# First batch's DFT stage on 64x64 tiles of TensorE, with its loads put in another order (spectral mixing followed by a tanh-shrink MLP)

## The chip, the cores and the metric

One Trainium2 chip, one core. The metric is the device time of one launch in microseconds, the median of several runs. Before the change it is 2542.09 us (three runs, 2541.68 to 2546.36).

## The reference

The input x has 8 batches of 3008 positions and 256 channels. Each batch is filtered along the positions in the frequency domain, and every resulting row then goes through an MLP whose nonlinearity is h - tanh(h):

```python
X = np.fft.rfft(x, axis=1)
Y = X * (filt_r + 1j * filt_i)[None, :, :]
y = np.fft.irfft(Y, n=3008, axis=1).reshape(8 * 3008, 256)
h = y @ w_in                      # 256 -> 2048
out = (h - np.tanh(h)) @ w_out    # 2048 -> 256
```

## The kernel before, in words

The DFT of length 3008 = 64 x 47 is done by matrix products. A position is 47 q + r, with q from 0 to 63. Stage one takes, for a residue r from 0 to 23, the 64 rows of x at r (lower partitions 0 to 63) and the 64 rows at 47 - r (upper partitions 64 to 127), and multiplies them by a table of cosines and sines. Stage two mixes the residues ("there", tiles `pq`, `pa`, `pb`), the filter is multiplied in (tiles `nn`, `xy`), and the way back (`pe`, `pu`) gives the rows that the MLP reads. Batch 0 does all of this in a prologue of some 76 us. The batches after it are prepared in steps that are put between the MLP's matmuls of the batch ahead of them, so that from there to the end TensorE has MLP work in a fixed order written out by the program.

The prologue's start is what the change touches:

- **Loads** (L1172 to L1187). For each of three chunks `c` of 8 residues there is a tile `xs[c]` of 128 partitions x 8 slots x 256 channels. SyncE's queue loads the table piece `fh` of chunk 0 and all lower halves; GpSimd's queue loads all upper halves but the first, which with the other two table pieces is on ScalarE's queue. Slot i of the upper half holds residue 47 - r, so it is read backwards from memory, one row of 1 KB at a time.
- **Table** (L1188, L1189). VectorE builds `f0`, 128 columns for each residue: the 64 columns of `fh`, and beside them the same columns with the sign of the upper rows turned.
- **Warmers** (L1200). 15 matmuls of 128x256 on a tile of ones, without use for the result.
- **Stage one** (`first0`, L1064 to L1074). For each residue and each half of the channels one full matmul: 128 rows (lower and upper at once), 128 channels as weights, 128 columns of `f0` moving. So the sum over lower and upper rows is made in the array, and the difference, which the sign in `f0` gives, too. Each PSUM bank of two residues is copied to the tile `turnt` (which is laid in the memory of `wd`), by ScalarE for ten of the twelve.
- **What follows.** `across(0)` (L1083 to L1100) transposes slices of `turnt`, over all residues, into `pq`; its first slice lies in the columns 64 to 127. ScalarE and VectorE then copy `pq`, and a row of VectorE work follows almost without a pause: conversion of the MLP's weights (L183 to L201, from a tile `raw`), the sums of stage two (L435, L436) and the filter (L447 to L456).
- **Filters.** GpSimd copies one element of `xs[2]` (`gate`, L1197), which waits for a piece of the last chunk, and only then issues the loads of the first filter tiles.

The loads of SyncE's and ScalarE's queues share eight completion counters in turn, so a later load of these queues is issued only when the load that had its counter before it has landed.

## Time and profile before

| what | time |
|---|---|
| median of three runs | 2542.09 us |
| the profiled execution's own time | 2542.18 us |
| its span, first to last instruction | 2540.3 us |
| TensorE busy in the span | 2522.6 us (99%) |
| granted TensorE clock, mean | 0.999 |
| first matmul of stage one | 10.72 us |
| first transpose behind stage one (`pq`) | 22.54 us |
| first matmul of the way back's last step (`pu`) | 76.05 us |

The span is 1.9 us less than the time of that execution. Times in rows of the trace are microseconds from the start of the span. An f32 matmul stands in the trace as two records on PE (and two on PEld, its weight loads), so 15 matmuls are 30 records.

### The profile page before, as it was taken

Reading aid. Unit: us, or ns where it says so; the run is one execution under the profiler, and the core shown is the slowest. Engines: PE = TensorE matmul, PEld = TensorE weight load, DVE = VectorE, ACT = ScalarE, POOL = GpSimd, SP = SyncE. Lnnn points to the kernel's source line nnn. Section 1 sums busy time; section 2 is a strip of 40 time slices with the busy share of each in tenths; the row PEclk is TensorE's granted clock in tenths of the full one; section 3 lists DMA queues with packets and bytes.
Section 4 is the critical chain, followed back from the end, with each engine's and each line's share of the span. In section 5 each row is a group of like instructions: output and inputs, shape, how many; then the busy total and the mean of one; then the engine's idle time right before and its main releaser. Section 6 shows DMA issues by size and latency. Waiting matters only on the chain.

```text
span 2540.3 us, 44575 instructions
## 1 busy us (share of the span) xinstructions
PE 2522.6 (99%) x17072; PEld 2173.1 (86%) x17072; DVE 1935.6 (76%) x2270; ACT 1694.2 (67%) x2551; POOL 1532.0 (60%) x1112
## 2 busy tenths in 40 slices
PE   9999999999999999999999999999999999999998
PEld 8678889888898888988888888898889888898887
DVE  6888877988678876888669886698866888555555
ACT  4666666667666766676667666666666666666665
POOL 5255665667556765676656665666655666455552
PEclk9999999999999999999999999999999999999999
DMA  9854224422343323342334322343123322110110
GB/s 245 261 150 117 65 54 100 112 65 53 86 108 91 82 69 89 80 112 59 80 87 105 87 56 72 96 111 89 36 72 84 92 66 53 26 31 19 25 22 19
DMA packets 333664, 211.37 MB, mean 83 GB/s; under 512 B 231645, under 2 KB 305531, under 8 KB 329793
## 3 DMA queue, kind: packets, MB, share of 16 engines
q1 hardware_dynamic: 319091, 184.93, 29.8%
q0 software_dynamic: 11120, 16.16, 2.3%
q10 hardware_dynamic: 3230, 7.34, 0.9%
q8 instruction: 136, 2.23, 0.4%
q14 instruction: 87, 0.71, 0.1%
HBM read 127.81 MB, written 83.39 MB: 83 GB/s over the span
## 4 chain that ended last, share of the span: by engine, by line
PE 96%; DVE 2%; DMA 1%; issue 0%; POOL 0%; ACT 0%; ACTq 0%; SPq 0%; POOLq 0%; DVEq 0%
PE o L821 44%; PE x L648 25%; PE z L648 12%; PE y L648 6%; PE pm L415 2%; PE pu L595 2%; PE pm L351 1%; PE o L883 1%; PE pf L308 1%; DMA filt<-in_filt_r_dram 1%; DMA x<-in_x_dram 0%; DMA ct<-e 0%; PE o L719 0%; PE x L719 0%; PE z L719 0%
## 5 line engine op out<-in xcount | busy, mean ns | idle before, releaser
L821 PE MATMUL o<-t,wd 128*128 128x256 f32 (+1 forms) x3008 | 762.7, 376 | 0.0
L619 POOL TENSOR_TENSOR t<-h 128x512 f32<-128x512 f32 (+1 forms) x184 | 303.6, 1650 | 707.3 <-DVE h L771 642.2
L771 DVE TENSOR_TENSOR h<-h,y 128x1024 f32<-128x1024 f32 (+1 forms) x384 | 571.0, 1487 | 156.4 <-ACT y L767 156.4
L821 PEld LDWEIGHTS o<-t,wd 128*128 128x128 f32 x3008 | 568.8, 190 | 84.5 <-POOL o L853 15.1
L648 PE MATMUL x<-tu,wu 128*128 128x256 f32 (+1 forms) x2256 | 571.4, 376 | 0.0
L821 PE MATMUL o<-h,wd 128*128 128x256 f32 (+1 forms) x2256 | 569.9, 375 | 0.2 <-DVE h L771 0.2
L648 PEld LDWEIGHTS x<-tu,wu 128*128 128x128 f32 x2256 | 427.4, 190 | 53.8 <-issue 3.9
L821 PEld LDWEIGHTS o<-h,wd 128*128 128x128 f32 x2256 | 428.3, 190 | 50.9 <-issue 0.8
L654 ACT COPY s<-x 128x512 f32<-128x512 f32 (+1 forms) x188 | 109.3, 581 | 517.4 <-PE x L648 517.3
L764 ACT ACTIVATE y<-y 128x1024 f32<-128x1024 f32 (+1 forms) x384 | 399.5, 1040 | 12.1
L767 ACT ACTIVATE y<-y 128x1024 f32<-128x1024 f32 (+1 forms) x384 | 399.8, 1041 | 4.6
L761 ACT ACTIVATE y<-h 128x1024 f32<-128x1024 f32 (+1 forms) x384 | 400.6, 1043 | 2.5 <-DVE h L697 1.7
L622 POOL TENSOR_TENSOR t<-h,t 128x512 f32<-128x512 f32 (+1 forms) x184 | 338.3, 1838 | 0.0
L620 POOL TENSOR_TENSOR t<-h,t 128x512 f32<-128x512 f32 (+1 forms) x184 | 310.5, 1688 | 14.4
L621 POOL TENSOR_TENSOR t<-h 128x512 f32<-128x512 f32 (+1 forms) x184 | 276.9, 1505 | 0.0
L654 ACT COPY u<-x 128x512 f32<-128x512 f32 (+1 forms) x376 | 214.1, 569 | 72.9 <-PE x L648 69.6
L697 DVE COPY h<-x 128x512 f32<-128x512 f32 (+1 forms) x188 | 127.6, 679 | 129.1 <-PE x L648 128.9
L689 DVE TENSOR_TENSOR h<-z,u 128x512 f32<-128x512 f32 (+1 forms) x188 | 127.2, 677 | 88.9 <-ACT u L654 88.5
L648 PE MATMUL x<-ut,wu 128*128 128x256 f32 (+1 forms) x752 | 194.0, 380 | 0.2 <-DVE h L697 0.2
L648 PE MATMUL z<-tu,wu 128*128 128x256 f32 (+1 forms) x752 | 190.2, 375 | 1.4 <-DVE h L705 1.4
L648 PE MATMUL y<-ut,wu 128*128 128x256 f32 (+1 forms) x752 | 190.1, 375 | 0.0
L648 PE MATMUL z<-ut,wu 128*128 128x256 f32 (+1 forms) x752 | 190.0, 375 | 0.0
(215 smaller groups left out, 2933.5 us busy)
## 6 DMA issues: line engine op xcount, KB each, us to landing
ft<-filt SPq DMA_DIRECT2D x28, 1024.0 KB
ct<-nn SPq DMA_DIRECT2D x56, 512.0 KB
e<-ct SPq DMA_DIRECT2D x47, 512.0 KB
a<-ct SPq DMA_DIRECT2D x112, 192.0 KB
out_dram<-ot SPq DMA_DIRECT2D x1248, 16.0 KB
x_sb<-in_x_dram SPq DMA_DIRECT2D x110, 128.0 KB
ct<-a SPq DMA_DIRECT2D x60, 128.0 KB
ct<-x_sb SPq DMA_DIRECT2D x60, 128.0 KB
```

The source lines that it names most:

```text
L619: by.tensor_sub(t[0], b[0][1], b[0][0])
L620: by.tensor_sub(t[1], b[1][1], t[0])
L621: by.tensor_sub(t[2], b[1][1], b[0][1])
L622: by.tensor_sub(t[3], b[1][0], t[1])
L648: nc.tensor.matmul(bank[:, k], wu[:, q - 1, (2 * u + k) * 128:(2 * u + k + 1) * 128], rhs[q - 1], start=(first and k == 0), stop=True, ski ...
L654: ACT.copy(t, X)
L697: V.tensor_copy(h[:, 2, :, 0:w], X)
L761: ACT.activation(y[k], ht[k], AF.Arctan, scale=TURN)
L764: ACT.activation(y[k], y[k], AF.Tanh, scale=BEND)
L767: ACT.activation(y[k], y[k], AF.Square, scale=SCALE, accum_out=y_sums[:, 2 * U + k // 2:2 * U + k // 2 + 1])
L771: V.tensor_mul(ht[k], ht[k], y[k])
L821: nc.tensor.matmul(product(q), wd[:, q - 1, (2 * u + k) * 128: (2 * u + k + 1) * 128], rhs[q - 1][:, k], start=(u == 0 and k == 0 and q == ...
```

## The change

Stage one of batch 0 works on quarters of the array. A matmul now has 64 rows, 64 channels as weights and 64 moving columns of `fh`; four of them, one in each quarter, take the place of one. The products of lower rows go to one PSUM bank and those of upper rows to another. ScalarE copies the upper bank to a tile `upper`, and VectorE writes sum and difference of the two to `turnt`. Since the upper rows are apart, slot 3 - k of an upper half can be paired with slot k of the lower half, so the upper halves are read forwards (3 or 4 KB at a time). The table is loaded as `fh`, 64 columns for each of the 24 residues; `f0` is left for the 8 residues that a later step of batch 1 needs, and built by ScalarE. The loads stand in the order of their use on SyncE's and ScalarE's queues, GpSimd loads no part of x any more, and `gate` looks at a piece that SyncE's queue loads. Six warmers stand ahead in place of 15, on ones in the memory of `wu`, and two more behind each half chunk but the last.

```diff
-                for i in range(0, 8, 2):
-                    r = 8 * c + i
-                    pf = z0("pf", [128, 2, 2, 128])
+                for at in (0, 4):
+                    r = 8 * c + at
+                    banks = [z0("pf", [128, 2, 4, 64]) for _ in range(2)]
                     for h in range(2):
-                        for k in range(2):
-                            nc.tensor.matmul(pf[:, h, k], xs[c][:, i + k, h * 128:h * 128 + 128],
-                                             f0[:, r + k], start=True, stop=True)
-                    copy = V.tensor_copy if c == 2 and i % 4 else ACT.copy
-                    copy(turnt[:, :, :, r:r + 2], pf.rearrange("p h k n -> p h n k"))
+                        for k in range(4):
+                            for bank, half, slot in zip(banks, rows, (at + k, at + 3 - k)):
+                                for m, part in enumerate(rows):
+                                    col = h * 128 + 64 * m
+                                    nc.tensor.matmul(bank[part, h, k],
+                                                     xs[c][half, slot, col:col + 64],
+                                                     fh[half, r + k], start=True, stop=True)
+                    if r < NH - 4:
+                        warmer(2, ones_t)
+                    t = tr.tile([128, 2, 4, 64], F32, tag="e1", bufs=2, name="upper")
+                    ACT.copy(t, banks[1])
+                    low, high = (v.rearrange("p h k n -> p h n k") for v in (banks[0], t))
+                    V.tensor_add(turnt[:, :, 0:64, r:r + 4], low, high)
+                    V.tensor_sub(turnt[:, :, 64:128, r:r + 4], low, high)
...
-                V.tensor_copy(f0[:, r:r + 8, 0:64], fh)
-                V.tensor_scalar(out=f0[:, r:r + 8, 64:128], in0=fh,
-                                scalar1=sgn, scalar2=None, op0=ALU.mult)
...
+            load_f(0, 8, nc.sync)
+            load_high(0, 0, ACT)
+            load_low(0, 0, nc.sync)
+            load_high(0, 4, ACT)
+            load_low(0, 4, nc.sync)
+            load_f(8, NH, ACT)
+            for k in (0, 4):
+                load_high(1, k, ACT)
+            for k in (0, 4):
+                load_low(1, k, nc.sync)
+            for k in (0, 4):
+                load_low(2, k, nc.sync)
+                load_high(2, k, nc.sync)
...
-            warmer(15, filt[2][:, 0])
+            warmer(6, ones_t)
             first0(0)
+            ACT.copy(f0[:, :, 0:64], fh[:, 0:8])
+            ACT.copy(f0[0:64, :, 64:128], fh[0:64, 0:8])
+            ACT.mul(f0[64:128, :, 64:128], fh[64:128, 0:8], -1.0)
             first0(1)
```

On TensorE, the program's start before the change reads as follows (`pf` is stage one's bank, `x_87`, `x_97`, `x_106` are the three chunks, `f_80` is `f0`; xN counts matmuls in a row):

```order
L1081 MATMUL warm<-filt_79 128x256 x15
L1071 MATMUL pf<-f_80,x_87 128x128 x16
L1071 MATMUL pf<-f_80,x_97 128x128 x16
L1071 MATMUL pf<-f_80,x_106 128x128 x16
L1094 MATMUL pq<-one_sb,wd 120x128 x8
```

And with the change, up to the second chunk (`x_85`, `x_86`, `x_87` are the chunks now):

```order
L1090 MATMUL warm<-wu 128x256 x6
L1074 MATMUL pf<-fh,x_85 64x64 x32
L1090 MATMUL warm<-wu 128x256 x2
L1074 MATMUL pf<-fh,x_85 64x64 x32
L1090 MATMUL warm<-wu 128x256 x2
L1074 MATMUL pf<-fh,x_86 64x64 x32
```

Nine warmers have gone from the front, ten stand between the half chunks, and each half chunk has 32 quarter matmuls where it had 8 full ones.

On VectorE, ahead of the first copy of `pq`, this stood last before the change:

```order
L1188 COPY f_80<-fh 128x8x64
L1189 TENSOR_SCALAR f_80<-fh,sgn 128x8x64
L1188 COPY f_80<-fh 128x8x64
L1189 TENSOR_SCALAR f_80<-fh,sgn 128x8x64
L1074 COPY wd<-pf 128x256x2 x2
L1099 COPY a_68<-pq 120x512
```

With the change the end of the same stretch is:

```order
L1082 TENSOR_TENSOR wd<-pf,upper 128x2x64x4
L1083 TENSOR_TENSOR wd<-pf,upper 128x2x64x4
L1082 TENSOR_TENSOR wd<-pf,upper 128x2x64x4
L1083 TENSOR_TENSOR wd<-pf,upper 128x2x64x4
L1108 COPY a_68<-pq 120x512
```

The building of the table has left VectorE, and for each half chunk a sum and a difference have come, twelve instructions in all (`wd` is the memory of `turnt`).

On SyncE's queue the loads of x and of the table now begin like this, where GpSimd had the upper halves before:

```order
L1183 DMA fh_81<-f 128x512
L1186 DMA x_85<-in_x_dram 64x1024 x2
L1186 DMA x_86<-in_x_dram 64x1024 x2
L1186 DMA x_87<-in_x_dram 64x1024
L1191 DMA x_87<-in_x_dram 64x1024
L1186 DMA x_87<-in_x_dram 64x1024
L1191 DMA x_87<-in_x_dram 64x1024
L1208 DMA one_sb<-one 128x128
L1209 DMA mats_sb<-mats 120x360
```

Two upper halves have come ahead of the identity `one_sb`, the matrices `mats_sb` and all that follows on this queue; the other upper halves stand on ScalarE's queue.

More of the change, by code (lines that the diff above doesn't have):

```diff
@@ L1162 @@
             filt = [pro.tile([KM, 4, DM], F32, name=f"filt{k}") for k in range(3)]
-            f0 = pro.tile([128, NH, 128], F32, name="f0")
+            f0 = pro.tile([128, 8, 128], F32, name="f0")
+            fh = pro.tile([128, NH, 64], F32, name="fh")
             warm_b = cst.tile([128, 1], F32, name="warm_b")
@@ L1166 @@
             jobs = parts_of((0, 1, 2, 4, 3, 5, 6, 7))
-            sgn = cst.tile([128, 1], F32, name="sgn")
-            for half in range(2):
-                V.memset(sgn[64 * half:64 * half + 64], 1.0 - 2 * half)
-            V.memset(filt[2][:, 0], 1.0)
-            xs, began = [], []
-            for c in range(3):
-                lo = int(c == 0)
-                xt = big([128, 8, DM], F32, "x0")
-                xs.append(xt)
-                fh = pro.tile([128, 8, 64], F32, tag="e1", bufs=4, name="fh")
-                (ACT if c else nc.sync).dma_start(fh, f_d[:, 512 * c:512 * c + 512])
-                if lo:
-                    V.memset(xt[64:128, 0], 0.0)
-                for k in (0, 4):
-                    nc.sync.dma_start(xt[0:64, k:k + 4], dram(x.tensor, (8 * c + k) * DM,
-                                                              [[NR * DM, 64], [1, 4 * DM]]))
-                    at = max(k, lo)
-                    (ACT if c + k == 0 else G).dma_start(
-                        xt[64:128, at:k + 4], dram(x.tensor, (NR - 8 * c - at) * DM,
-                                                   [[NR * DM, 64], [-DM, k + 4 - at], [1, DM]]))
-                r = 8 * c
-                V.tensor_copy(f0[:, r:r + 8, 0:64], fh)
-                V.tensor_scalar(out=f0[:, r:r + 8, 64:128], in0=fh,
-                                scalar1=sgn, scalar2=None, op0=ALU.mult)
@@ new lines, with load_f, load_low @@
+            ones_t = wu[:, 6, 0:256]
+            V.memset(ones_t, 1.0)
+            xs, began = [big([128, 8, DM], F32, "x0") for _ in range(3)], []
+            V.memset(xs[0][64:128, 3], 0.0)
+            def load_f(a, b, queue):
+                queue.dma_start(fh[:, a:b], f_d[:, 64 * a:64 * b])
+            def load_low(c, k, queue):
+                queue.dma_start(xs[c][0:64, k:k + 4], dram(x.tensor, (8 * c + k) * DM,
+                                                           [[NR * DM, 64], [1, 4 * DM]]))
@@ new lines, in load_high @@
+            def load_high(c, k, queue):
+                n = 4 - (c + k == 0)
+                queue.dma_start(xs[c][64:128, k:k + n],
+                                dram(x.tensor, (NR - 8 * c - k - 3) * DM,
+                                     [[NR * DM, 64], [1, n * DM]]))
+            load_f(0, 8, nc.sync)
[6 more added lines that the diff above has]
+                load_high(1, k, ACT)
```

## Prediction

> **What bounds the kernel now.** I read the page first (its head, the busy shares and the chain that ended last), then a table of four stretches.

> ```profile
> span 2540.3 us, 44575 instructions
> PE 2522.6 (99%) x17072; PEld 2173.1 (86%) x17072; DVE 1935.6 (76%) x2270; ACT 1694.2 (67%) x2551; POOL 1532.0 (60%) x1112
> PE 96%; DVE 2%; DMA 1%; issue 0%; POOL 0%; ACT 0%; ACTq 0%; SPq 0%; POOLq 0%; DVEq 0%
> ```

> The chain is TensorE nearly all the way. The table says where it isn't (columns: PE, PEld, DVE, ACT, POOL busy, clock, DMA share, GB/s):

> ```profile
> 24.00:40.00 16.00, 14.93 (x82) 12.37 (x82) 15.45 (x25) 8.90 (x16) 6.87 (x11) 1.00 0.84 222
> 40.00:56.00 16.00, 15.33 (x78) 12.86 (x79) 15.19 (x21) 6.87 (x13) 12.32 (x15) 1.00 0.84 233
> 56.00:76.00 20.00, 17.62 (x90) 15.08 (x88) 17.65 (x32) 7.74 (x15) 1.67 (x3) 1.00 0.69 227
> 76.00:2440.00 2364.00, 2362.08 (x16208) 2034.59 (x16209) 1826.42 (x2108) 1603.35 (x2413) 1461.54 (x1029) 1.00 0.33 81
> ```

> From 76 to 2440 us TensorE is busy for 2362.08 of 2364 us, on work whose order is fixed. So whatever the prologue wins or loses by 76 us moves the end by as much. From 24 to 56 us VectorE is busy for 30.6 of 32 us: an earlier first copy of `pq` pulls that whole row of work forward, if its data are there. The question is then when `pq` begins, and whether that lead lives to 76 us. The timeline of the start (start, us, engine, line):

> ```profile
> 1.45 9.44 PE L1081 MATMUL warm<-filt 120*128 120x256 f32 x30 [1.45 <-DVE filt L1170]
> 10.72 10.88 PE L1071 MATMUL pf<-f,x 128*128 128x128 f32 x96
> 19.96 1.58 ACT L1074 COPY wd<-pf 128x512 f32<-128x512 f32 x2 [1.10 <-PE pf L1071]
> 21.64 0.80 DVE L1074 COPY wd<-pf 128x512 f32<-128x512 f32 x1 [0.99 <-PE pf L1071]
> 22.54 1.06 PE L1094 MATMUL pq<-one_sb,wd 128*120 128x128 f32 x8 [0.94 <-ACT wd L1074]
> ```

> Warmers until 10.7 us, stage one's 96 records without a gap until 21.6, one last copy of 0.80 us, then `pq` at 22.54. In that stretch TensorE sets the pace, not the loads:

> ```profile
> 2.00:4.00 2.00, 2.00 (x6) 1.58 (x5) 0.00 (x0) 1.35 (x2) 2.00 (x5) 1.00 0.97 258
> 4.00:6.00 2.00, 2.00 (x6) 1.53 (x6) 1.36 (x2) 0.13 (x1) 2.00 (x4) 1.00 0.95 206
> 6.00:8.00 2.00, 2.00 (x9) 1.68 (x8) 0.00 (x0) 0.00 (x0) 0.48 (x2) 1.00 1.03 294
> 8.00:10.00 2.00, 2.00 (x11) 1.77 (x10) 0.00 (x0) 0.00 (x0) 0.00 (x0) 1.00 1.01 291
> 10.00:12.00 2.00, 2.00 (x17) 1.90 (x16) 0.82 (x2) 0.18 (x1) 0.00 (x0) 1.00 1.05 304
> 12.00:14.00 2.00, 2.00 (x21) 2.00 (x20) 0.00 (x0) 1.81 (x3) 0.00 (x0) 1.00 1.04 291
> 14.00:16.00 2.00, 2.00 (x21) 2.00 (x20) 0.82 (x2) 1.80 (x3) 0.60 (x2) 1.00 1.06 264
> ```

> Two things are to be seen. The same warmer goes at 6 records in 2 us at first and at 11 later, though the clock column shows 1.00: TensorE starts at half pace. The chain has the later pace of matmuls with 256 columns:

> ```profile
> 41.33 0.43 PE pe L1139 x2
> ```

> That is 0.215 us a record, and 0.43 at half of it. 12 cold and 18 warm records make 5.2 + 3.9 = 9.1 us, and 0.2 for the first one the 9.27 us from 1.45 to 10.72: the pace turns near 6.7 us. And the DMA engines are full (share near 1); two microseconds times each GB/s give 0.52, 0.93, 1.52, 2.10, 2.71, 3.29, 3.82 MB moved by 4, 6, 8, 10, 12, 14 and 16 us.

> **The change, part by part.**

> *Start.* The warmers wait for a memset of VectorE as before, a little earlier; six are 12 records at the cold pace, 12 x 0.43 = 5.2 us with 0.1 to 0.2 for the first, from 1.2 to 6.5 us. The first half chunk needs the table piece and the first two x pieces:

> ```profile
> 4.20 0.62 DVE L1188 COPY f<-fh 128x512 f32<-128x512 f32 x1 [2.42 <-DMA fh<-f]
> 6.82 0.33 SPq L1191 DMA_DIRECT2D one_sb<-one  x1
> 15.40 0.19 POOL L1197 COPY gate<-x 1x1 f32<-1x1 f32 x1 [8.91 <-DMA x<-in_x_dram]
> ```

> The table piece had landed by 4.20. The load of `one_sb` had to wait for the counter of the first lower half, so that one landed by 6.8. In the new order it has the same place behind the same piece, so I take 6.8 us for stage one's start, where it was 10.72.

> *Matmuls.* Quarters of the same shape run later in this kernel:

> ```profile
> 110.83 1.67 PE L719 MATMUL x<-ut,wu 128*128 128x448 f32 x4
> 112.33 1.67 PE L883 MATMUL o<-h,wd 128*128 128x448 f32 x4
> ...
> 118.57 1.67 PE L719 MATMUL o<-ut,wu 128*128 128x448 f32 x4
> 120.17 1.16 PE L595 MATMUL pu<-gt,e 64*64 64x64 f32 x64
> 121.26 1.77 PE L883 MATMUL o<-h,wd 128*128 128x448 f32 x4
> ```

> 64 records, 32 quarter matmuls, from 120.17 to the next group at 121.26 are 1.09 us, and 0.1 at the way in (1.60 from the start of the group before it, where its like at 110.83 has 1.50): 1.18 us, which is one half chunk. It had 8 full matmuls, 16 of the 96 records in 10.88 us, 1.81 us. Two warmers are 4 x 0.215 = 0.86 us. So a half chunk with its warmers is 2.04 us, and six of them less the last warmers are 11.4 us, where the 96 records took 10.9: the quarters save 3.8 us and the ten warmers give 4.3 back. The lead is that of the start.

> *Loads.* x and the table are 3.87 MB, and nothing else is on the queues before the last of them but what I name below. If SyncE's and ScalarE's queues share evenly, the second chunk's first half needs the fourth load of ScalarE's queue, 1.25 MB on that queue and 2.49 MB in all: 11.3 us on the table above, where TensorE would be there at 6.8 + 2 x 2.04 = 10.9. It waits 0.4 us. The next halves need all 1.51 MB of ScalarE's queue and as much of SyncE's (3.0), then SyncE's seventh load (3.3) and all 3.87 MB: 13.0, 14.2 and 16.2 us, where TensorE comes at 13.3, 15.4 and 17.4. So they don't wait, and stage one ends at 17.4 + 1.2 = 18.6 us (before: 21.6). Reading forwards makes larger packets; in the rows, the GB/s don't show me a gain beyond that from 258 to 304, worth some 0.3 us on the half megabyte that had 1 KB packets on ScalarE's queue, and I count nothing.

> *Evacuation.* The tail behind the last matmul grows: a copy by ScalarE, then a sum and a difference by VectorE, where it was one copy. The rows of the like steps (min/median/max ns):

> ```profile
> L601 ACT COPY odd<-pu x48: 577/586/588, 77.9 to 2463.8; 128x512 f32<-128x512 f32 x48
> L605 DVE TENSOR_TENSOR ut<-pu,odd x11: 690/692/693, 78.6 to 2464.4; 128x512 f32<-128x512 f32 x11
> L605 DVE TENSOR_TENSOR ut<-even,odd x37: 864/1506/1751, 215.7 to 2101.8; 128x512 f32<-128x512 f32 x37
> L606 DVE TENSOR_TENSOR ut<-even,odd x37: 1214/1756/1764, 217.0 to 2103.3; 128x512 f32<-128x512 f32 x32, 128x384 f32<-128x384 f32 x5
> ```

> With one operand in PSUM, as here, 0.69 us. The writes to `turnt` go in short runs, and the copy that wrote there so took 0.80 (the timeline above), so I take 0.75, with 0.69 and 1.76 (both operands in SBUF) as the ends. Tail: 0.59 + 0.05 + 2 x 0.75 = 2.1 us, against 0.80. Ahead of the last half, VectorE's 1.5 us fits under the 2.04 us that TensorE takes, and so do ScalarE's 0.59 us and its three builds of `f0` (some 1.8 us between the second and the third copy, which has 2.5 us of room by the waits above; without the room, the third sum would come some tenths late, which two halves later is made good). VectorE is rid of building the table, which cost nothing beside the loads.

> *Sum.* Stage one ends at 18.6, the copy starts 0.15 later, tail to 20.9, `pq` at 21.0: **1.5 us earlier** than 22.54.

> *What is late next.* The waits table of the first 60 us has two that lie on the way:

> ```profile
> POOL filt L1122 <- DMA filt<-in_filt_r_dram: 3.0, 1, 3.0
> ACT top L181 <- DMA raw<-in_moe_w_in_dram: 0.9, 1, 0.9
> ```

> Both are for loads that come earlier now. The gate opens on a piece that by the sum above lands near 14.2 us, not 15.40, so the first filters are asked for 1.2 us earlier; GpSimd also has its five issues of x off its queue. The second weight load is issued by ScalarE behind four copies of stage one, near 15 us, not behind eight. On SyncE's queue `one_sb`, `mats_sb`, the first weight load and the third filter stand behind three more loads, but wait for counters that turn earlier. So I let the lead of 1.5 us through whole. The profiled execution is 2542.18 us, 1.9 over its span and 0.1 over the median; 2542.18 - 1.5 = 2540.7, and **2540.6 us** on the median's scale.

> **The rivals.**

> *The lead is used up by loads* (0.24). For it: the DMA engines are full until past 16 us, and the weight load and filters that now start earlier share them with the last pieces of x. If the last piece lands at 18.4 us, two microseconds later than my sum, stage one ends at 19.6, `pq` begins at 22.0, and 0.5 us is left: 2541.6; with a filter late by another microsecond or two, 2543.5. Against it: SyncE's queue issues the last x piece ahead of its own later loads.

> *More is won than the start* (0.14). The two waits above, and those for DMAs between 56 and 76 us, where TensorE lacks 2.4 of 20 us, shrink because the loads come earlier: up to 1.5 + 0.9 + 2.4 = 4.8 us, 2537.4, and a little beyond with a wait that I don't see. Against it: VectorE, not the loads, is busy from 24 to 56 us.

> *Slower: TensorE stays at its cold pace* (0.05). Six warmers end just where the pace turned before, and short quarters with waits between may not hold it. Then a half chunk takes 2.36 and its warmers 1.71 us: 6.8 + 5 x 4.07 + 2.36 = 29.5 in place of 18.6 us, `pq` at 31.9, 9.4 us late: 2551.5. It decides once the cold pace lasts some 3 us beyond the sixth warmer, since 3 us of work at half pace cost the lead. Against it stands a pause later in the prologue:

> ```profile
> 76.05 0.33 PE L595 MATMUL pu<-gt,e 64*64 64x64 f32 x4 [2.42 <-DMA e<-ct]
> 76.71 1.15 PE L595 MATMUL pu<-gt,e 64*64 64x64 f32 x60 [0.34 <-issue]
> ```

> After 2.42 us without a matmul, 60 quarter records take 1.15 us, the warm pace. My longest pause is 2.4 us, ahead of `pq`. [...]

> *Slower: VectorE becomes the bound* (0.04). If sum and difference cost 1.51 and 1.76 us as in the rows with both operands in SBUF, six pairs from 8.7 us on end at 28.3, `pq` at 28.4: 5.9 us late, 2548. The point is 1.02 us each, where a pair reaches TensorE's 2.04. [...] The 690 ns row speaks against it here.

> *Slower: the change doesn't do what it says, the quarters don't run side by side* (0.03). One after another, a 64-column record can't be faster than half of a 128-column one, 0.057 us: 3.6 us a half chunk, stage one's end at 32.5, 12.4 us late, 2554.6. The row of 64 records in 1.16 us has the same shape, so this is nearly excluded.

> **How the numbers follow.** The forecast (2539.4 to 2541.6 us) has 0.50, the lead used up 0.24, more won 0.14, the three slow cases 0.12. About 0.2%, 5.1 us, is what a measurement of this kernel can tell from no change: faster than 2537.0 takes about half of "more won", 0.08; slower than 2547.2 are the slow cases, 0.12; within it 0.80. These two tails are the 2 in 10 that the range leaves out, so its low end is 2537.0; its high end is 2544.5, the end of the lead used up with a microsecond for the spread of the runs (up to 2546.36 before).

> **What would show it.** In the profile after: stage one's first matmul near 6.8 us and its last near 18.4; 64 records of it in some 1.1 us; the sums at 0.69 to 0.80 us; `pq` near 21.0; `pu` near 74.5, and the rest as it was. A first matmul past 8 us, gaps over 1 us ahead of half chunks four to six, records at twice the time, or a `pu` that has not moved with `pq` would each make the prediction wrong, at the step that it names.

## The result, and the profile after

The changed kernel takes 2551.70 us (median of seven runs, 2551.05 to 2553.01), where the kernel before takes 2542.09 (seven runs on the same chip): by the means 1.0033 times as long, with an interval of 1.0022 to 1.0045. By the medians it is 9.6 us slower; forecast were 1.5 us less. The profiled execution, by which what follows is read, took 2552.22 us with a span of 2550.3, so 10.0 more than before. The page's head, the chain, and four stretches (PE, PEld, DVE, ACT, POOL busy, clock, DMA share, GB/s); the rows of before stand in the prediction, but for the first stretch, whose row of before comes last here:

```profile
span 2550.3 us, 45158 instructions
PE 95%; DVE 2%; DMA 2%; issue 1%; ACT 0%; ACTq 0%; POOL 0%; SPq 0%; POOLq 0%; DVEq 0%
```

```profile
20.00:24.00 4.00, 1.39 (x16) 1.08 (x8) 2.69 (x3) 0.59 (x1) 3.35 (x6) 0.80 1.07 286
24.00:40.00 16.00, 12.42 (x114) 9.92 (x113) 8.78 (x13) 5.64 (x10) 5.70 (x10) 0.73 0.70 190
56.00:76.00 20.00, 19.96 (x105) 17.06 (x104) 18.92 (x30) 8.53 (x16) 9.22 (x12) 1.00 0.86 272
76.00:2440.00 2364.00, 2358.87 (x16193) 2031.08 (x16192) 1829.22 (x2114) 1599.03 (x2408) 1455.00 (x1025) 1.00 0.34 82
```

```profile
20.00:24.00 4.00, 2.67 (x23) 2.26 (x21) 1.81 (x3) 2.34 (x4) 1.04 (x3) 1.00 1.07 253
```

Two things are new. The chain now has "issue" in it, and the clock column, 1.00 in every stretch of before, falls to 0.80 and 0.73 between 20 and 40 us. Where it happens, the timeline of TensorE shows (start, us, engine, line, tiles, records, and in brackets the idle time ahead and what ended it):

```profile
6.02 1.16 PE L1074 MATMUL pf<-fh,x 64*64 64x64 f32 x64
...
8.96 1.16 PE L1074 MATMUL pf<-fh,x 64*64 64x64 f32 x64 [0.72 <-DMA x<-in_x_dram]
...
13.01 1.15 PE L1074 MATMUL pf<-fh,x 64*64 64x64 f32 x60 [1.07 <-DMA x<-in_x_dram]
...
15.15 0.33 PE L1074 MATMUL pf<-fh,x 64*64 64x64 f32 x5
16.88 1.14 PE L1074 MATMUL pf<-fh,x 64*64 64x64 f32 x59 [1.40 <-issue]
17.95 1.13 PE L1090 MATMUL warm<-wu 128*128 128x256 f32 x4
19.02 1.16 PE L1074 MATMUL pf<-fh,x 64*64 64x64 f32 x64
22.79 2.08 PE L1090 MATMUL warm<-wu 128*128 128x256 f32 x4 [2.61 <-issue]
24.79 1.60 PE L1074 MATMUL pf<-fh,x 64*64 64x64 f32 x64
29.19 1.92 PE L1103 MATMUL pq<-one_sb,wd 128*120 128x128 f32 x8 [2.80 <-issue]
...
84.93 0.33 PE L595 MATMUL pu<-gt,e 64*64 64x64 f32 x4 [2.00 <-DMA e<-ct]
```

The quarters do run side by side: 64 records in 1.16 us, where one after another would take 3.6 by the prediction's estimate. But TensorE stops twice within stage one, 1.4 and 2.6 us long, and nothing that it could have waited for ends these stops. The first falls amid a half chunk whose loads had all landed by 14.81 us, the second ahead of warmers, which read only a tile of ones. Behind the second stop, four records of warmers take 2.08 us where they took 1.13, and `pq` 1.92 where before had 1.06: half pace.

`pq` begins at 29.19 us and not at 22.54 (6.65 later), `pu` comes 55.74 us behind it and not 53.51 (2.2), and the rest of the span is 2465.4 us and not 2464.2 (1.1). This is the 10.0 us. The last piece falls at 148.97 us: there TensorE waits 1.46 us for a copy by ScalarE (`u`, L654), which stands behind another copy that waits 3.13 us for a transfer (`ct<-a`). At the same place before (138.23 us) TensorE has no wait, and the transfer holds the copy for 0.84 us. From 153 us on the steps of the MLP keep 10.4 us behind before, and the end gives 0.4 back.

Against the forecast of 21.0 for `pq`, 8.2 us are missing: the load of the second chunk's first half (13.01, forecast 11.3) 1.7; the first stop (16.88, where 15.15 was due) 1.7; the second (22.79, where the warmers were due at 20.1) 2.7; half pace in the warmers and the last half chunk behind it 1.4 (2.08 and 1.60 for 1.13 and 1.16); the tail behind the last matmul, 2.8 for 2.4, 0.4; these make 7.9, and 0.3 is spread over the groups.

Two things can be counted in the trace beside the rows. TensorE's records (weight loads, matmuls, its few semaphore instructions), counted from the start, give the place of each stop in the program, and the queue that the page calls "instruction" moves packets of 16,384 bytes:

```text
kernel          last start, next start    records so far
changed         15.26 -> 16.88 us         449
changed         19.96 -> 22.78 us         705
16 KB packets of the instruction queue, changed kernel: at 14.13 (1.26 us), 20.00 (1.18 us)
before: 262 records by 22 us, first such packet at 20.53
whole trace, such packets and records of TensorE: before 136 and 34,355, changed 138 and 34,935
```

449 and 705 are 256 apart, and over the whole trace there are 253 records for each packet, in both kernels. An estimate from the two: one packet brings 256 instructions, 64 bytes each. So the first theory, argued from these rows, is **supply**: TensorE's instructions come through the DMA engines in blocks of 256; while x fills these engines (share 1.01 to 1.07 from 4 to 24 us), a block takes longer to come than quarter matmuls take to use it up (3.08 us for the 256 records from 16.88 to 19.96), four instructions for a matmul that lasts 0.04 us (32 in 1.16). Before had 192 instructions in all of stage one, the changed kernel has 768. The second, **clock**: the stops cost the pace, and the half pace a part of the rest. The rivals are the parts of the change that the prediction named: the loads on two queues, the evacuation by VectorE, the early start.

### The profile page after: what moved, and what is told of

It reads as the page before. It is cut to its first block, busy times and chain, and to the rows that moved or that the text cites. A ratio compares the mean times of both kernels' runs of the same rounds, so it can differ in the third digit from the quotient of the medians.

```text
span 2550.3 us, 45158 instructions
## 1 busy us (share of the span) xinstructions
PE 2524.4 (99%) x17362; PEld 2171.3 (85%) x17362; DVE 1943.6 (76%) x2272; ACT 1691.3 (66%) x2550; POOL 1526.6 (60%) x1107
## 4 chain that ended last, share of the span: by engine, by line
PE 95%; DVE 2%; DMA 2%; issue 1%; ACT 0%; ACTq 0%; POOL 0%; SPq 0%; POOLq 0%; DVEq 0%
PE o L821 44%; PE x L648 25%; PE z L648 12%; PE y L648 6%; PE pm L415 2%; PE pu L595 2%; DMA ct<-a 1%; PE pm L351 1%; DMA x<-in_x_dram 0%; PE pe L1150 0%; PE pe L1148 0%; PE o L883 0%; PE pf L308 0%; DVE h L771 0%; DMA filt<-in_filt_r_dram 0%
## 5 line engine op out<-in xcount | busy, mean ns | idle before, releaser
L654 ACT COPY s<-x 128x512 f32<-128x512 f32 (+1 forms) x188 | 109.3, 581 | 516.5 <-PE x L648 516.5
L654 ACT COPY u<-x 128x512 f32<-128x512 f32 (+1 forms) x376 | 214.1, 569 | 72.9 <-PE x L648 69.1
```

The costliest lines, as they stand in the source:

```text
L654: ACT.copy(t, X)
```

## The experiments

**An early start alone.** The kernel before with six warmers, nothing else changed.

```diff
-            warmer(15, filt[2][:, 0])
+            warmer(6, filt[2][:, 0])
```

> The kernel before, with 6 warmers in place of 15 and nothing else changed: it tells what the early start is worth without quarters and without the new order of loads. Theory F (TensorE runs out of instructions: they arrive in blocks of 256, and stage one on quarters uses up a block in some 6 us): no change of the instruction count that matters (about 220 TensorE instructions to the end of stage one, under the first limit of 449), so no pause without a releaser; stage one begins at 6.5 to 9 us and pq at 20.5 to 22, the total is 0.5 to 2 us under before. Theory L (the loads set the pace, and an early start only waits for them): stage one starts early but waits between chunks, pq at 21.5 to 22.5, the total within 1 us of before. Neither expects a loss over 2 us; a loss would be by the halved clock after waits for loads.

```profile
5.96 2.02 PE L1071 MATMUL pf<-f,x 128*128 128x128 f32 x16 [0.18 <-DMA x<-in_x_dram]
10.87 10.80 PE L1071 MATMUL pf<-f,x 128*128 128x128 f32 x80 [2.89 <-DMA x<-in_x_dram]
22.60 1.06 PE L1094 MATMUL pq<-one_sb,wd 128*120 128x128 f32 x8 [0.93 <-ACT wd L1074]
```

2542.82 us (10 runs), ratio 0.9998 (0.9989 to 1.0008): no difference. Stage one begins at 5.96 us, waits 2.89 us for x, and `pq` is where it was. The 15 warmers of before stand in front of little that could go earlier with these loads: the pieces of x that land at 12.97, 15.35 and 17.70 us leave stage one's end at some 21.3 us even at before's pace (an estimate; 21.6 before). The trace has a second loss here, behind the wait: the clock records show half pace from 11.30 to 14.71 us, but most of that is hidden by these loads. The forecast's whole lead was that of the start.

**The loads alone.** The kernel before with the changed order of loads on two queues (upper rows still read backwards), full matmuls, six warmers; the table pieces in tiles of their own.

```diff
...
+            load_f(0, nc.sync)
+            load_high(0, 0, ACT)
+            load_low(0, 0, nc.sync)
...
-            warmer(15, filt[2][:, 0])
+            warmer(6, filt[2][:, 0])
```

> The kernel before with the new order and queues of the loads and 6 warmers, but with full matmuls, so upper halves still read backwards and the table built by VectorE. Theory F: as the instruction count is that of before, no pause without a releaser; pq at 20 to 21.5, total 1 to 2.5 us under before (2539.5 to 2541). Theory L: the last pieces of x land later than before (19 us or more, against 18.3), stage one waits for them, pq at 23 or later, and a good part of the 9.6 us loss is seen here (over 2544).

```profile
9.75 2.05 PE L1071 MATMUL pf<-f,x 128*128 128x128 f32 x16 [1.39 <-DMA x<-in_x_dram]
14.26 9.01 PE L1071 MATMUL pf<-f,x 128*128 128x128 f32 x64 [2.46 <-DVE f L1205]
24.20 1.06 PE L1094 MATMUL pq<-one_sb,wd 128*120 128x128 f32 x8 [0.93 <-ACT wd L1074]
```

2545.37 us (10 runs), ratio 1.0008 (0.9998 to 1.0018). `pq` comes 1.66 us late, and no idle row marked issue stands in stage one. The waits for x and the table use up the early start, and the pace behind them makes the lateness: the clock records show half pace from 15.46 to 18.87 us, and the 64 records take 9.01 us where before's pace (96 in 10.88) would make 7.25. By the ratio the new loads cost some 2 of the 9.6 us, and within the interval perhaps nothing. The loads themselves were slower in the new order on two queues: 202 to 242 GB/s between 6 and 14 us, where the kernel with six warmers, with the loads of before, moved 280 to 290.

**More instructions alone.** The kernel before, with nine of its warmers replaced by 128 quarter matmuls (512 instructions) on the tile of ones, which have no use.

```diff
-            warmer(15, filt[2][:, 0])
+            warmer(6, filt[2][:, 0])
+            for _ in range(4):
+                idle = [z0("idle", [128, 4, 2, 64]) for _ in range(2)]
+                for k in range(8):
...
+                            nc.tensor.matmul(bank[part, k // 2, k % 2], ones_t[half, 64 * m:64 * m + 64],
...
```

> The kernel before with the last 9 of its 15 warmers replaced by 128 quarter matmuls on ones, which take about the same time (4.4 us against 3.9) but are 512 instructions in place of 36; loads, stage one and evacuation are untouched. Theory F: TensorE stops after 449 instructions, inside the quarter warmers, and again after 705, inside stage one, each time for 1 to 4 us without a releaser, with the fetch of a block seen in the time before; pq 3 to 8 us later than before, total 2545 to 2551. Theory L: nothing changes but 0.5 us, total 2542 to 2543.

```profile
6.07 3.36 PE L1208 MATMUL idle<-wu 64*64 64x64 f32 x211
14.77 1.55 PE L1208 MATMUL idle<-wu 64*64 64x64 f32 x45 [5.34 <-issue]
16.25 12.21 PE L1071 MATMUL pf<-f,x 128*128 128x128 f32 x96
29.39 1.06 PE L1094 MATMUL pq<-one_sb,wd 128*120 128x128 f32 x8 [0.93 <-ACT wd L1074]
```

2549.58 us (8 runs), ratio 1.0028 (1.0017 to 1.0039). Matmuls that wait for no load and no other engine stop for 5.34 us, exactly behind record 449 again. `pq` is 6.85 us late: the stop, and half pace up to 18.85 us behind it. The expected stop at 705 did not come: by then only stage one's full matmuls use instructions, and slowly (192 records in 12.21 us). So added instructions make the stop here, in a kernel that has the loads and the stage one of before.

**The same with quiet DMA engines.** The kernel before, with 256 useless quarter matmuls (1024 instructions) at the very end.

```diff
+            for tags in ("xy", "zt") * 4:
+                idle = [ps.tile([128, 4, 2, 64], F32, tag=tag, bufs=1, name="idle") for tag in tags]
...
+                            nc.tensor.matmul(bank[part, k // 2, k % 2], one[half, 64 * m:64 * m + 64],
...
```

> The kernel before with 256 quarter matmuls (1024 TensorE instructions) without use put at its very end, where the DMA engines are nearly idle (share 0.09 in the last 100 us before). It is the disputed cost by itself, in a quiet place. Theory F, with the fetch delayed by full DMA engines: a block of 256 comes in time or nearly so, pauses of under 0.5 us per block, about 16 us for all of them and 14 to 17 us more in total. Rival (the fetch itself takes some 5 us whatever the DMA engines do): pauses of 1 to 3 us at each of four limits, 20 to 27 us more in total.

```profile
2539.22 3.14 PE L1492 MATMUL idle<-one_sb 64*64 64x64 f32 x198 [0.21 <-DVE ot L929]
2544.11 2.10 PE L1492 MATMUL idle<-one_sb 64*64 64x64 f32 x128 [1.75 <-issue]
2547.58 2.10 PE L1492 MATMUL idle<-one_sb 64*64 64x64 f32 x128 [1.38 <-issue]
2551.05 1.04 PE L1492 MATMUL idle<-one_sb 64*64 64x64 f32 x54 [1.38 <-issue]
```

2556.98 us (4 runs), ratio 1.0047 (1.0031 to 1.0064). The rows restart at 2544.11, 2547.58 and 2551.05: 3.47 us for each block of 256 instructions (128 matmul records and as many weight loads), of which 2.10 are work. So even at the end, where the DMA engines have a mean busy share of 0.14 (2538 to 2557 us), a block takes 3.5 us. My expectation of less than 0.5 us a pause fell; the pauses are those of the rival. While the DMA engines were full (share 1.01 to 1.07), a block took 5.9 us in the changed kernel (from 16.88 to 22.78). Most of the difference lies ahead of the block's packet: counted from the end of the stop before it, the packet begins 1.05 us later in quiet (2547.58 to 2548.63) and 3.1 us later under the loads (16.88 to 20.00), and takes 0.98 and 1.18 us.

**The quarters with the loads of before.** The changed kernel with the three queues and the backward reads of before, 15 warmers ahead and none between.

```diff
...
-                    if r < NH - 4:
-                        warmer(2, ones_t)
...
-            warmer(6, ones_t)
+            warmer(15, ones_t)
```

> The other half of the change alone: stage one on quarters with sum and difference by VectorE, but with the loads of before (their order, queues and backward reading) and its 15 warmers ahead, none between. Theory F (blocks of 256 TensorE instructions run out): TensorE stops without a releaser after 449 instructions, at the end of the third half chunk near 14 us, and after 705, 1 to 4 us each; pq at 25.5 to 29 in place of 22.54, total 3 to 8 us over before. Theory L (it was the new order of loads): with the old loads pq comes at 22 to 23.5 and the total is within 1.5 us of before.

```profile
17.68 3.77 PE L1074 MATMUL pf<-fh,x 64*64 64x64 f32 x127 [4.01 <-issue]
23.50 1.40 PE L1074 MATMUL pf<-fh,x 64*64 64x64 f32 x65 [2.05 <-issue]
29.23 1.93 PE L1101 MATMUL pq<-one_sb,wd 128*120 128x128 f32 x8 [4.33 <-issue]
```

2552.62 us (5 runs), ratio 1.0040 (1.0026 to 1.0054): as slow as the whole change, with stops behind 449 and 705 records again. 127 records take 3.77 us, where 128 had taken 2.10 at 9.45 us; the clock records have half pace there (14.62 to 21.45 us). The loss comes with the quarters, without the new loads.

**Unstepped reads.** The changed kernel with the banks laid out so that ScalarE and VectorE read without a stride.

```diff
-                    banks = [z0("pf", [128, 2, 4, 64]) for _ in range(2)]
+                    banks = [z0("pf", [128, 2, 64, 4]) for _ in range(2)]
...
```

> The changed kernel with the PSUM banks of stage one laid out so that the four residues lie next to each other: the matmuls write with a step, and ScalarE and VectorE read both operands in order; the writes to the transposed tile stay as they are. It tells whether the 1.02 us of sum and difference (0.69 in the like rows) come from the stepped reads. If so, 0.69 to 0.80 us each, pq 0.4 to 0.6 us earlier; if they come from the short runs of the writes, 1.0 us as before. Theory F expects the pauses without releaser at 449 and 705 instructions unchanged, and the total within 1.5 us of the changed kernel.

The last sums, first of the changed kernel, then of this one:

```profile
27.13 1.02 DVE L1082 TENSOR_TENSOR wd<-pf,upper 128x512 f32<-128x512 f32 x1 [3.71 <-ACT upper L1080]
```

```profile
27.44 0.69 DVE L1082 TENSOR_TENSOR wd<-pf,upper 128x512 f32<-128x512 f32 x1 [5.31 <-ACT upper L1080]
```

2551.58 us (6 runs), ratio 1.0034 (1.0021 to 1.0046). The stride was worth 0.33 us a sum; `pq` comes 0.35 us earlier (28.84), and no gain shows in the time. Two sums would have made 0.66, but in this profile half pace held on from 22.24 to 35.89 us, and the last half chunk took 1.99 us (1.60 in the changed kernel). The stop at 705 is there with 2.61 us; at 449 the next record comes only 0.29 us later, since a wait for x stands just ahead. VectorE had been idle for 3.71 us ahead of the last pair in the changed kernel: between half chunks it was not the bound.

**Work behind the last half chunk.** The changed kernel with six more warmers there, so that TensorE does not idle while the sums are made.

```diff
-                    if r < NH - 4:
-                        warmer(2, ones_t)
+                    warmer(2 if r < NH - 4 else 6, ones_t)
```

> The changed kernel with six more warmers behind the last half chunk, ahead of pq, where TensorE waits 2.8 us for the last sum and difference. They take 2.6 us of that wait. Theory C (the pauses cost a second time, by the halved clock): the clock record shows no half pace from 29.2 to 36.0 us any more, pq stays at 29 to 30, the way from pq to pu goes back from 55.7 to 53.5 us, and the total is 1.5 to 2.5 us under the changed kernel. Without theory C the total stays within 0.5 us of it, or rises by the warmers.

```profile
25.72 2.86 PE L1089 MATMUL warm<-wu 128*128 128x256 f32 x12
28.62 1.06 PE L1102 MATMUL pq<-one_sb,wd 128*120 128x128 f32 x8
...
82.14 0.33 PE L595 MATMUL pu<-gt,e 64*64 64x64 f32 x4 [2.24 <-DMA e<-ct]
```

2549.57 us (9 runs), ratio 1.0029 (1.0019 to 1.0039). More work for TensorE, and 2.1 us less time by the medians (the two intervals overlap): `pq` takes 1.06 us again, and `pu` comes 53.5 us behind it as before the change, not 55.7. That piece of the loss was the clock. A new one came at `pu`: half pace from 83.66 to 87.08 us, behind the pause of 2.24. Eight of the 13 traces have such a stretch at `pu`, those of before and of the change have none.

**Half the instructions.** The changed kernel with 64x128 tiles: each pair of quarters with the same rows in one matmul.

```diff
-                                for m, part in enumerate(rows):
-                                    col = h * 128 + 64 * m
-                                    nc.tensor.matmul(bank[part, h, k],
+                                nc.tensor.matmul(bank[:, h, k],
...
```

> The changed kernel with tiles of 64 rows x 128 columns in place of 64 x 64 (one matmul for all 128 channels of a half), so stage one has half as many TensorE instructions (about 450 with its warmers instead of 830), with the same loads, order and evacuation. Theory F: no pause of over 1 us without a releaser inside stage one (the first limit of 449 falls at its very end), pq 4 to 6 us earlier than in the changed kernel (23 to 25 instead of 29.2), total 2543 to 2547. Theory L or a theory that evacuation sets the pace: the loads and the evacuation are the same, so pq stays near 28 to 29 and the total at 2550 to 2552.

```profile
19.04 2.00 PE L1072 MATMUL pf<-fh,x 64*128 64x64 f32 x32
20.97 1.13 PE L1088 MATMUL warm<-wu 128*128 128x256 f32 x4
22.03 2.00 PE L1072 MATMUL pf<-fh,x 64*128 64x64 f32 x32
26.81 1.51 PE L1101 MATMUL pq<-one_sb,wd 128*120 128x128 f32 x8 [2.77 <-issue]
```

2551.92 us (6 runs), ratio 1.0053 (1.0032 to 1.0075), with runs from 2548.05 (the profiled one) to 2563.93. The stops within stage one are gone, as supply has it, but `pq` (26.81) and the time are later than I expected: a half chunk now takes 2.00 us in place of 1.16, and the idle time behind the last one, while the sums are made (2.77 us), is followed by a slow `pq` once more (1.51 us, 1.06 before). The spread I could not explain at this point.

**A version without any of the faults named so far.** 64x128 tiles, unstepped reads, one warmer between half chunks, four behind the last.

```diff
-                    banks = [z0("pf", [128, 2, 4, 64]) for _ in range(2)]
+                    banks = [z0("pf", [128, 2, 64, 4]) for _ in range(2)]
...
-                    if r < NH - 4:
-                        warmer(2, ones_t)
+                    warmer(1 if r < NH - 4 else 4, ones_t)
```

> The changed kernel with four edits: each quarter pair put back into one 64x128 tile (half the TensorE instructions), banks laid out so that VectorE and ScalarE read them without a stride, one warmer between half chunks instead of two, four behind the last one. Theory, instruction supply first and its clock loss second: TensorE gets its instructions in blocks of 256, a block takes 5 to 8 us while the loads run, and the changed kernel used one up in 4 to 5 us; with the stage below 449 instructions no idle row marked issue of 1 us or more stands in it, it is bounded by the loads (last half landed near 19.1 us in the changed kernel), its last block ends between 20.5 and 21.5 us; with no pause there and warm work behind the last half chunk, no half-pace stretch between 20 and 36 us; the sums take 0.69 us each, as in the kernel with unstepped reads; pq starts at 23.0 to 23.8 us, pu near 76.5 to 77.5, and the time is 2542.5 to 2544.5 us, 7 to 9 us under the changed kernel. Rival, that the loss lies in the two-halves scheme itself (copies, sums, load order on two queues) and not in the instruction count: pq stays at 27 us or later and the time at 2549 us or more.

Timeline, and then the stretches (PE busy, clock, DMA share, GB/s):

```profile
7.17 2.00 PE L1072 MATMUL pf<-fh,x 64*128 64x64 f32 x32 [0.83 <-DMA x<-in_x_dram]
9.10 1.12 PE L1087 MATMUL warm<-wu 128*128 128x256 f32 x2
10.15 3.68 PE L1072 MATMUL pf<-fh,x 64*128 64x64 f32 x32
...
29.19 3.68 PE L1072 MATMUL pf<-fh,x 64*128 64x64 f32 x32
```

```profile
9.20:36.50 27.30, 27.30 (x179) 0.50 0.97 255
```

2555.02 us (6 runs, 2547.64 to 2556.99), ratio 1.0038 (1.0026 to 1.0050): no better than the change, and by the median 3.3 us worse. My expectation fell. No stop is there, as expected, but TensorE is busy for 27.30 of 27.30 us and at half pace all the time. So idle time isn't what the clock goes by in this run, and "the pause costs the pace" was the wrong way to put it.

The clock's records turn at multiples of 3.41 us from one another (in the changed kernel at 5.32, 22.39, 25.80, 29.21 and 36.04 us). I counted for each such stretch the matmul work in it: columns streamed, times the share of the 128x128 array that is in use, times 0.84 ns (0.215 us for 256 columns of a full matmul). (The expectations of the next two runs count each record where it starts; here it is split at the border of a stretch. So this version's first stretch has 1.29 there and 1.24 here. The 1.56 that is given there as the least ahead of full pace does not come out: the changed kernel's stretch from 22.39 had 1.34.) Over the first 100 us of all 13 traces (the two experiments below among them) these are 381 stretches:

```text
kernel, stretch                   idle us   work us   the next stretch runs at
changed       15.57 to 18.98      1.32      1.62      full pace
changed       18.98 to 22.39      2.21      0.89      half
changed       25.80 to 29.21      2.80      0.39      half
half tiles    13.62 to 17.04      0.00      1.88      full
this version   5.83 to  9.24      0.83      1.24      half
this version  16.06 to 19.48      0.00      0.92      half
wide warmers  20.91 to 24.32      1.75      1.35      full
all: followed by half (41)    idle from 0.00    work up to 1.32
all: followed by full (340)   idle up to 1.76   work from 1.29
```

By idle time the two groups overlap from 0.00 to 1.76 us; by work they part at 1.3 us of 3.41, but for one stretch of 1.29 that full pace followed and one of 1.32 that half pace followed, of which any border has one on its wrong side. It takes the whole share to part them: counted by the tile's rows alone at least 11 of the 381 stretches are on the wrong side of any border, by its columns alone 19, without a share 21. So the theory of the clock, for the stretches of these traces, became: **the pace follows the work of the stretch before, counted by the share of the array.** A 64x64 matmul counts for a quarter in it. This version's first stretch had 1.24, and by an estimate its pattern gives no more than 1.0 at half pace (0.92 in the row from 16.06), so by this theory it could not get out until the four warmers at the end.

**Three warmers more ahead.** The same version; the added warmers fill the wait of 0.83 us and the first stretch.

```diff
-            warmer(6, ones_t)
+            warmer(9, ones_t)
```

> The kernel of the previous run (64x128 tiles, unstepped reads, one warmer between half chunks, four behind the last) with nine warmers ahead of stage one in place of six. The previous run refuted the theory that its fewer instructions would mend the time: it had no pause, yet ran at half pace from 9.24 to 36.55 us and took 2555 us. New theory: the pace of a stretch of 3.41 us is set by the matmul work of the stretch before it, counted by the share of the array that it fills and at full pace, not by idle time. Worked out so from the records of all runs (columns streamed x share of the array x 0.84 ns), stretches with 1.29 us of work or less were followed by half pace and those with 1.56 or more by full pace; the previous run's first stretch had 1.29, with 0.83 us of idle time, and its half-pace stretches 0.97, which kept it there. With three warmers more the first stretch has 2 us or more, and the later ones about 1.7: no half-pace stretch before 36 us, blocks of 2.0 us and warmers of 0.57 in all of stage one, its last block ends at 22.0 to 22.6, pq at 24.1 to 24.8, time 2543.3 to 2545.5 us. Rival: narrow tiles can't hold the pace however the stage begins, or the phase of the stretches decides: half pace as before, 2553 us or more, or runs in two groups.

```profile
8.07 2.00 PE L1072 MATMUL pf<-fh,x 64*128 64x64 f32 x32
...
20.87 2.00 PE L1072 MATMUL pf<-fh,x 64*128 64x64 f32 x32
22.81 1.99 PE L1087 MATMUL warm<-wu 128*128 128x256 f32 x8
24.98 1.06 PE L1100 MATMUL pq<-one_sb,wd 128*120 128x128 f32 x8 [0.18 <-issue]
```

2547.58 us (12 runs), ratio 1.0025 (1.0015 to 1.0035); the profiled run 2545.96. With three warmers more the median is 7.4 us shorter, though one of the six runs without them took 2547.64 us too. In the profile, all of stage one runs at full pace, 2.00 us a half chunk, as the theory of work says. The time is some 2 us over the expected range; over 1 us of it, in the profile, is half pace from 78.52 to 81.94 us, behind the pause ahead of `pu` (2.05 us later than before at `pu`, 3.2 at 93 us). Three of the twelve runs took 2554.8 to 2555.5 us at a mean clock of 0.994 to 0.995, the others 2544.1 to 2548.7 at 0.997 to 0.999. So the rival has a part: in some runs the pace is lost still. That the phase of the stretches against the program does it is my guess, here and for the spread of the half tiles; no such run was profiled, so it is not shown.

**Wider warmers.** The changed kernel with its quarters; warmers of 512 columns, and two behind the last half chunk too.

```diff
-                    if r < NH - 4:
-                        warmer(2, ones_t)
+                    warmer(2, wu[:, 6, 0:512])
...
```

> The changed kernel with its two warmers between half chunks twice as wide (512 columns, same number of instructions), and two behind the last half chunk as well. Theory of work in each stretch of 3.41 us: a half chunk now brings 0.86 + 1.72 = 2.6 us of work in about 2.9 us, so that a pause of 1 to 2 us for instructions no longer takes a stretch under 1.3 us of work; no half-pace stretch between 5 and 40 us, stage one's last block ends at 23.5 to 24.5, pq at 26.3 to 27.3, pu 53.5 us behind it, time 2545.8 to 2547.5 us: 4.5 to 6 us under the changed kernel though TensorE has more to do. Rival, that only the pauses for instructions count and the clock is a by-product: the pauses after 449 and 705 instructions are still there, the added warmers (0.86 us in each of six half chunks) come on top, and the time is that of the changed kernel or more, 2551.5 us or above.

```profile
20.15 1.16 PE L1074 MATMUL pf<-fh,x 64*64 64x64 f32 x64
23.07 1.98 PE L1089 MATMUL warm<-wu 128*128 128x512 f32 x4 [1.75 <-issue]
24.98 1.16 PE L1074 MATMUL pf<-fh,x 64*64 64x64 f32 x64
...
86.47 0.48 PE L595 MATMUL pu<-gt,e 64*64 64x64 f32 x4 [4.95 <-DMA e<-ct]
```

2550.83 us (6 runs, 2548.60 to 2554.55, the profiled one), ratio 1.0030 (1.0018 to 1.0042). The stop behind record 705 is there, with 1.75 us, and the pace behind it is full (four records of 512 columns in 1.98 us, a half chunk in 1.16), as the theory of work says of a stretch with 1.35 us. The time was missed: the wider warmers take most of what they save, the last half chunk ends at 26.1 us and not by 24.5, a stretch with 1.25 us of work behind it costs the pace at 31.15, and this run waits 4.95 us for `e`, a load, ahead of `pu`. Why that load is late I did not find.

None of these versions beats the kernel before. The loads leave little to win in front of `pq`. In the changed kernel the last piece of x lands at 19.14 us; with a half chunk (1.16) and its tail (2.8) behind it, `pq` cannot begin before some 23.1, later than the 22.54 of before. In the kernel before it lands at 18.33; a half chunk of full matmuls (1.81) behind it would end at some 20.1, where stage one ends at 21.6, so 1.5 us is the most that an earlier start could win there. Both are estimates from these rows.

## Why the prediction was wrong

- *The frame held:* what the prologue loses reaches the end. 8.9 us by `pu` are 10.0 in the span, and the 1.1 between them are lost at one wait, at 148.97 us.
- *Start* (6.8 us): 6.02. Even earlier, and worth nothing that shows, as the early start alone told. The forecast counted it as the lead, but the lead existed only if the later loads came as summed.
- *Matmuls* (1.18 us for 64 records, "a half chunk with its warmers is 2.04 us"): **the step that failed.** The burst is 1.16 us, as read. But the row that I took it from was one burst of 32 matmuls among full matmuls, and I used it as a pace for 192 in a row. What one matmul costs to supply, four instructions, was counted nowhere, and no rival had it. The kernel with the added instructions alone shows it with neither the loads nor the sums of the change; the two stops put the changed kernel 4.4 us behind the forecast, the largest part of the 8.2 that `pq` is late against it, and the half pace behind them 1.4.
- *Loads* (11.3, 13.0, 14.2, 16.2): the second chunk's first half began at 13.01, 1.7 us late, and the last piece landed at 19.14. I summed the GB/s of before, 291 to 304 between 6 and 14 us; the changed kernel's two queues moved 244 to 272. Reading forwards did not make up for the new order on two queues: there the backward reads moved 202 to 242 (the loads alone). And the sum left out more than the rate: for the kernel before it would have said 16.2 as well, where the last piece landed at 18.33. The rows:

```profile
6.00:8.00 2.00, 2.00 (x69) 1.70 (x68) 0.13 (x1) 0.59 (x1) 0.00 (x0) 1.00 1.04 244
8.00:10.00 2.00, 1.28 (x66) 1.02 (x64) 1.87 (x2) 0.00 (x0) 0.00 (x0) 1.00 1.04 256
12.00:14.00 2.00, 0.99 (x60) 1.02 (x60) 0.80 (x1) 0.45 (x1) 0.00 (x0) 1.00 1.03 272
```

- *Evacuation* (0.75 a sum): 1.02, for the stepped reads; unstepped it is 0.69. With 1.02 us it stood just at the point that the prediction gave, but TensorE was slower still, so between half chunks it did not decide. In the tail it did add 0.4 us, and taking the 0.33 us a sum away brought `pq` 0.35 us forward and no gain that shows in the time.
- *Rival, cold pace* (0.05, 2551.5 us): its time was nearly the one measured, its mechanism only in part. TensorE did come to full pace, at 5.32 us by the clock records; it lost it at 22.39 and 29.21 us, behind stretches with 0.89 and 0.39 us of work. What I held against it was the pause of the next point, as long as my longest (2.42 and 2.4 us), with full pace behind it. Here stretches with 2.21 and 0.83 us of idle time were followed by half pace, and others with none at all, while one with 1.75 was followed by full pace. What parts the stretches in these traces is the work counted by the share of the array in use, at about 1.3 us. That the rival's time came so near the measured one is luck.
- *The pause of 2.42 us ahead of `pu`*, which I took as evidence that such a pause is harmless, fell on two stretches; the one with more of it, 1.58 us, still had 1.66 us of work. The row had not shown that.
- *Shown and not shown:* that added instructions make the stops is shown (5.34 us behind record 449), and that little work in a stretch goes with half pace behind it (41 stretches, with up to 1.32 us). That one packet brings 256 of TensorE's instructions is an estimate from counts. That the blocks are late because of the DMA engines is argued, from 3.5 us a block in quiet against 5.9 and the packets of the instruction queue. That the work is what sets the pace is a theory: the count parts the 381 stretches at about 1.3 us but for one, and what it said came true in two profiles (three warmers more, wider warmers); a run that changes the work of one stretch and nothing else was not made. Why the transfer behind the wait at 148.97 us is late in the changed kernel stays open.

## What to carry to other kernels

Where a matmul is cut into smaller ones, count TensorE's instructions per microsecond beside its busy time: here a block of 256 took 3.5 us in quiet (DMA share 0.14) and 5.9 under full loads (1.01 to 1.07), and a stage that used 256 in 3.08 us stopped, whatever its matmuls cost. A pace read from a short burst was no pace for a long row (1.18 us forecast for 64 records, and stops of 1.4 and 2.6 us among them), and a start that was made earlier was worth what the last load left of it (stage one at 5.96 in place of 10.72 us, and a ratio of 0.9998). Small tiles also went with half pace here (64x128 tiles, busy for 27.30 of 27.30 us): ask of each stretch, 3.41 us in these traces, how much of the full array's work is in it, not how much of it is busy.
